# Ordering the engine queues of a linear-attention + MLP kernel with another scheduling model of the framework

## The chip, the cores and the metric

The kernel runs on one core of a Trainium2 chip. The metric is the device time of one execution, in microseconds (us). Before the change three runs gave 836.24, 839.51 and 843.57 us, a median of 839.51 us. The profile that is read below is of one more execution of the same kernel.

## The reference

Per batch and head (4 x 8 of them, head size 40) a 40 x 40 state is carried over 768 steps. The attention output then goes, as 3072 tokens of 320 numbers, through an MLP with 2048 hidden units and the function h * tanh(softplus(h)).

```python
for t in range(S):
    y[:, :, t] = np.einsum('bhd,bhde->bhe', rt, state)
    Sa = np.einsum('bhde,bhe->bhd', state, at)
    state_decay = state * wt[:, :, None, :] - np.einsum('bhd,bhe->bhde', Sa, bt)
    state = state_decay + np.einsum('bhd,bhe->bhde', vt, kt)
...
h = x @ w_in
g = h * np.tanh(softplus(h))
return g @ w_out
```

## The kernel before

The 768 steps are cut into 12 chunks of 64. Inside a chunk the recurrence becomes matrix products and the inverse of a triangular matrix, so that only the state goes from chunk to chunk. The text below uses these names:

- **P c.b** (`pre_a`, L128 to L203), the preparation of half b of chunk c, 24 in all. SyncE (SP) loads `wa` (L131) and `bk` (L134), each into one of two buffers, so P of two units later waits until the buffer is free. VectorE (DVE) forms running products of the decay: a reduction L145, a reciprocal L146, a scan L147, L150, L152, L156, a scan back L157, and L170, which scales `bk`. TensorE (PE) multiplies (L186) and transposes (L202); ScalarE (ACT) and DVE empty the results (L188 to L191, L193).
- **I n** (L209 to L220), the inversion for two chunks at a time, six in all, I0 to I5. It is one chain of 64 DVE instructions: a transpose L209, thirty pairs L214/L216, each of which needs the pair ahead of it, a transpose L218 that gives `TT`, and L220.
- **J n** (L232 to L260), what follows it on PE: 32 x 32 products L232 and L241, ACT copies into `bdT` (L249 to L251), and the products L258 that ACT copies into `KT` (L260). The chunks 2n and 2n+1 need J n.
- **a, b, u, d, c** of a chunk, the step itself, for two groups of heads: a is L277 to L286 (`pu`, with `KT`), b is L314/L316, u L293, d L304, and c is L334, L339 (`pq`), L342 and L346 (the new state) and L343 (the output `yev`).
- **W 0 to W 19**, the conversion of one piece of the MLP's weights. SP loads the piece into `cv_d` (L453), ACT makes `cv_m` (L459), DVE runs L461 to L463, ACT makes the high part `w_ih` or `w_oh` (L494) and DVE the low part `w_il` or `w_ol` (L495). W0 to W11 are `in_wi`, with one buffer for `cv_d` in all; W12 to W19 are `in_wo`. The last five, W15 to W19, have two buffers for `cv_d`.
- **X i** (L472 to L476, L565 to L568), the loads of MLP input i (`xy` and `xp`, one buffer each) and its split into `xh` (ACT, L566) and `xl` (DVE, L567, L568); **m i** (L583, L585, L588, L589), the first product of the MLP with its activation; **M i** (L603 to L605), the second product, which for token block 0 needs all of W12 to W19 in turn.

All of this is written in program order inside one `TileContext`. When the context is left, the framework's scheduler simulates the engines and decides the order in which each engine's instructions stand in its queue. Each engine then takes its queue strictly in that order; an instruction whose inputs aren't there holds up what is behind it, and so does a DMA issue on SP or POOL. The program gives the scheduler hints, `tc.high_priority(offset=...)`, from the table `OFF` for each piece of work:

```python
def at(tc, k):
    return tc.high_priority(offset=OFF[k]) if OFF.get(k) else nullcontext()
...
ORDER = '0aiA1'
```

`ORDER` is the program order for two chunks: step 2n, P of two pairs ahead, I and J of the next pair, at the end the weights, step 2n+1. Buffer counts (such as `NWA = 2` for `wa` and `bk`, `NXP = 1` for `xy` and `xp`, `CVC = 2` for the last `cv_d`) are constants at the head of the file.

Of the kernel before, what the change touches and what calls it, by code (L numbers as in the profile page):

```python
# [47 lines left out]
def layouts(inp, S=768):  # L48
    nch = S // C

    def v(x):
        return x[:, :, :S].reshape(4, 2, 2, 2, nch, C, 40)

    r, k, vv, w, a, b = (v(inp[n]) for n in 'rkvwab')
    o = {}
    wt = w.transpose(4, 2, 1, 6, 3, 0, 5).reshape(nch, 2, 2, 40, 8, C)
    wa = np.zeros(wt.shape[:4] + (1040,), np.float32)
    wa[..., :520].reshape(wt.shape[:4] + (8, 65))[..., 1:] = wt
    wa[..., 528:] = a.transpose(4, 2, 1, 6, 3, 0, 5).reshape(nch, 2, 2, 40, 512)
    o['wa'] = wa  # L60
    bt, kt = (x.transpose(4, 2, 1, 6, 3, 0, 5).reshape(nch, 2, 2, 40, 8, 1, C) for x in (b, k))
    bk = np.concatenate([bt, kt], -2)
    bk[:, 1] = np.concatenate([kt, bt], -2)[:, 1]
    o['bk'] = bk.reshape(nch, 2, 2, 40, 8, 128)
    o['rD'] = np.ascontiguousarray(r.transpose(4, 1, 6, 2, 3, 0, 5)).reshape(nch, 2, 40, 16, C)
    o['vD'] = np.ascontiguousarray(vv.transpose(4, 1, 6, 3, 0, 2, 5)).reshape(nch, 2, 40, 8, 128)
    o['vN'] = np.ascontiguousarray(vv.transpose(4, 2, 5, 3, 0, 1, 6)).reshape(nch, 2, C, 16, 40)
    p = np.arange(128)
    cst = np.zeros((128, 328), np.float32)
    cst[:, :128] = np.eye(128)  # L70
    cst[:, 128:192] = (p[:, None] % 64) < np.arange(64)
    cst[:, 192:256] = np.arange(64) < (p[:, None] // 64) * 32 + p[:, None] % 32
    cst[:, 256:296] = (p[:, None] % 64) == np.arange(40)
    cst[:, 296:328] = np.arange(32) < p[:, None] % 32
    o['cst'] = cst
    return o
# [356 lines left out]
def mlp_layouts(inp):  # L433
    wi, wo = inp['moe_w_in'], inp['moe_w_out']
    wi = wi.reshape(2, 2, 2, 40, 2048).transpose(1, 3, 0, 2, 4).reshape(320, 2048)
    a = np.empty((128, 3, 2048), wi.dtype)
    a[:, 0], a[:, 1] = wi[0:128], wi[128:256]
    a[0:64, 2] = a[64:128, 2] = wi[256:320]
    o = {'wi': a.reshape(128, 3, 4, 512).transpose(0, 2, 1, 3), 'wo': wo.reshape(16, 128, 320).transpose(1, 0, 2)}
    o = {n: np.ascontiguousarray(x).reshape(128, -1) for n, x in o.items()}  # L440

    return {n: x.view(np.int64) if x.dtype == np.float64 else x for n, x in o.items()}
# [185 lines left out]
def build(tc, I, out, nch):  # L628
    with ExitStack() as ctx:
        dp = ctx.enter_context(tc.tile_pool(name="dp", bufs=1, space=bass.MemoryType.DRAM))  # L630
        yD = dp.tile([nch, 2, 40, 2, 512], F32, name="yD")
        pD = dp.tile([nch, 2, 40, 2, 520], F32, name="pD")
        M = Mlp(ctx, tc, I, yD, pD, out)
        with ExitStack() as actx:
            attention(actx, tc, I, yD, pD, nch, M)
        M.run(nch)


def launch(**inputs):
    import concourse.bacc as bacc  # L640
    import concourse.tile as tile
    from concourse.bass_utils import run_bass_kernel_spmd

    nch = inputs['r'].shape[2] // C
    arrays = layouts(inputs, nch * C)
    arrays.update(mlp_layouts(inputs))
    nc = bacc.Bacc("TRN2", target_bir_lowering=False, num_devices=1)
    I = {n: nc.dram_tensor("in_" + n, x.shape, mybir.dt.from_np(x.dtype), kind="ExternalInput").ap() for n, x in arrays.items()}
    out = nc.dram_tensor("out_0", (nch * 256, 320), F32, kind="ExternalOutput").ap()
    with tile.TileContext(nc) as tc:  # L650
        build(tc, I, out, nch)
    res = run_bass_kernel_spmd(nc, [{"in_" + n: x for n, x in arrays.items()}], core_ids=[0]).results[0]["out_0"]
    return np.ascontiguousarray(res.reshape(nch, 4, C, 320).transpose(1, 0, 2, 3)).reshape(nch * 256, 320)
# [4 lines left out]
```

## Time and profile before

| | before |
|---|---|
| runs | 836.24, 839.51, 843.57 us |
| median | 839.51 us |
| profiled execution, first to last instruction | 843.5 us |
| PE, PEld, DVE, ACT, POOL busy | 748.6, 695.6, 462.0, 429.0, 103.3 us |
| mean granted TensorE clock | 0.939 |

The page gives no time of the profiled execution beside its span of 843.5 us. PE is the matmul part of TensorE and PEld its weight loads, which run beside the matmuls. An f32 matmul of the program leaves two records in the trace (the counts after x), one of the MLP, in another format, leaves one. In a timeline row the first number is the start in us, the second the length, and what stands in brackets is the idle time of the engine just before and what ended it. The table of stretches gives the busy time of each engine in it and then the clock that TensorE was granted (1.00 is full speed), the busy share of the DMA engines and GB/s.

### The profile page before, as it was taken

The page shows a single profiled execution, that of the slowest core. Times are in us where ns is not written, and L with a number is a line of the kernel's source. Part 1 is how long each engine was busy: PE and PEld are TensorE (multiplying, and loading weights), DVE is VectorE, ACT ScalarE, POOL GpSimd, SP SyncE. Part 2 cuts the span into 40 slices and gives each one's busy share as a digit, 9 for nine tenths or more (in the row PEclk, how much of TensorE's full clock was granted, in tenths as well). Part 3 has the DMA queues.
Part 4 walks back from the last instruction along what each step waited for, and adds up shares of the span by engine and source line. Part 5 has one row for each costly group of instructions (what it writes and reads, how often), then busy time and mean ns, then how long its engine had stood idle before and what let it go on. Part 6 is the DMA issues. An engine that isn't in the chain of part 4 may idle for free.

```text
span 843.5 us, 18796 instructions
## 1 busy us (share of the span) xinstructions
PE 748.6 (89%) x7816; PEld 695.6 (82%) x7816; DVE 462.0 (55%) x975; ACT 429.0 (51%) x937; POOL 103.3 (12%) x182
## 2 busy tenths in 40 slices
PE   2645898998989889889799899999999999999998
PEld 2534697887868778778768799999999999999998
DVE  6789879739899658788924639221222222122110
ACT  4533647774586866566738546333333333333331
POOL 8100012113122023221101200000000000000000
PEclk9855689899999999899959999999999999999999
DMA  6422223323423233323425734211120111100000
GB/s 177 134 71 64 74 63 73 90 67 105 129 81 80 66 88 103 82 67 96 123 66 142 179 109 128 54 35 36 38 54 25 31 54 35 35 21 16 16 1 32
DMA packets 58212, 61.91 MB, mean 73 GB/s; under 512 B 25536, under 2 KB 48704, under 8 KB 58128
## 3 DMA queue, kind: packets, MB, share of 16 engines
q1 hardware_dynamic: 49296, 40.94, 17.6%
q0 software_dynamic: 8832, 19.79, 9.5%
q8 instruction: 61, 1.00, 0.5%
q14 instruction: 23, 0.19, 0.1%
HBM read 48.79 MB, written 11.86 MB: 72 GB/s over the span
## 4 chain that ended last, share of the span: by engine, by line
PE 62%; DVE 15%; ACT 15%; issue 5%; DMA 2%; ACTq 0%; DVEq 0%; SPq 0%
PE ph L583 21%; PE po L604 7%; PE po L605 7%; PE po L603 7%; PE pa L186 5%; PE pa L258 4%; PE pq L314 3%; PE pq L334 2%; DVE XL L216 2%; DVE tmp L214 2%; ACT ad L155 2%; PE pu L284 1%; DMA cv_d<-in_wo 1%; DVE P L147 1%; ACT bdT L250 1%
## 5 line engine op out<-in xcount | busy, mean ns | idle before, releaser
L583 PE MATMUL ph<-xh,w_ih 128*128 128x256 f32 x576 | 148.3, 283 | 0.5 <-ACT xh L566 0.5
L585 ACT ACTIVATE g<-ph 128x512 f32<-128x512 f32 x96 | 57.3, 598 | 179.3 <-PE ph L583 179.2
L589 DVE TENSOR_TENSOR gl<-g,gh 128x1024 fp32r<-128x1024 f32 x48 | 58.7, 1225 | 160.7 <-ACT gh L588 160.4
L583 PE MATMUL ph<-xh,w_il 128*128 128x256 f32 x576 | 123.6, 283 | 0.0
L186 PE MATMUL pa<-bk,ad 128*128 128x168 f32 x384 | 85.0, 373 | 42.7 <-DVE bk L170 15.0
L604 PE MATMUL po<-w_ol,gh 128*128 128x320 f32 x384 | 118.8, 310 | 0.1
L605 PE MATMUL po<-w_oh,gl 128*128 128x320 f32 x384 | 118.4, 309 | 0.0
L603 PE MATMUL po<-w_oh,gh 128*128 128x320 f32 x384 | 117.7, 309 | 0.0
L186 PEld LDWEIGHTS pa<-bk,ad 128*128 128x128 f32 x384 | 70.8, 233 | 47.8 <-issue 22.8
L583 PEld LDWEIGHTS ph<-xh,w_ih 128*128 128x128 f32 x576 | 109.3, 190 | 0.7 <-ACT xh L566 0.7
L583 PE MATMUL ph<-xl,w_ih 128*128 128x256 f32 x384 | 101.2, 285 | 0.0
L583 PEld LDWEIGHTS ph<-xh,w_il 128*128 128x128 f32 x576 | 96.3, 190 | 0.0
L583 PEld LDWEIGHTS ph<-xl,w_ih 128*128 128x128 f32 x384 | 73.1, 190 | 0.8 <-issue 0.5
L604 PEld LDWEIGHTS po<-w_ol,gh 128*128 128x128 f32 x384 | 72.1, 188 | 0.5 <-DVE w_ol L495 0.5
L605 PEld LDWEIGHTS po<-w_oh,gl 128*128 128x128 f32 x384 | 72.1, 188 | 0.1
L603 PEld LDWEIGHTS po<-w_oh,gh 128*128 128x128 f32 x384 | 71.8, 188 | 0.0
L258 PE MATMUL pa<-bdT,HA 128*104 128x128 f32 x384 | 57.0, 304 | 9.0 <-ACT bdT L251 7.3
L258 PEld LDWEIGHTS pa<-bdT,HA 128*104 128x104 f32 x384 | 49.9, 190 | 14.4 <-ACT bdT L251 9.1
L216 DVE TENSOR_TENSOR XL<-XL,tmp 128x30 f32<-128x30 f32 (+9 forms) x180 | 59.0, 328 | 2.4
L214 DVE TENSOR_TENSOR tmp<-XL 128x30 f32<-128x30 f32 (+9 forms) x180 | 58.5, 325 | 2.5
L314 PE MATMUL pq<-bdr,UVT 128*128 128x128 f32 x384 | 57.3, 294 | 2.3 <-DVE UVQ L316 1.5
L314 PEld LDWEIGHTS pq<-bdr,UVT 128*128 128x128 f32 x384 | 50.8, 205 | 4.0 <-DVE UVQ L316 1.9
(89 smaller groups left out, 1243.5 us busy)
## 6 DMA issues: line engine op xcount, KB each, us to landing
wa<-in_wa SPq DMA_DIRECT2D x48, 162.5 KB
bk<-in_bk SPq DMA_DIRECT2D x48, 160.0 KB
cv_d<-in_wi SPq DMA_DIRECT2D x12, 512.0 KB
cv_d<-in_wo SPq DMA_DIRECT2D x8, 640.0 KB
pD<-P POOLq DMA_DIRECT2D x48, 81.2 KB, 2.2
VS<-in_vN POOLq DMA_DIRECT2D x24, 160.0 KB, 3.6
UVT<-in_vD POOLq DMA_DIRECT2D x24, 160.0 KB, 3.9
bdr<-in_rD POOLq DMA_DIRECT2D x24, 160.0 KB, 4.4
```

The source lines that it names most:

```text
L155: A.copy(ad[q, :, :, al], a[q].rearrange("p (s k t) -> p s k t", k=2, t=32))
L186: PE.matmul(pt[:, j], ad[:, s0 + j].rearrange("p k a t -> p (k a t)"), bk[:, s0 + j], start=(j == 0), stop=True, skip_group_check=True)
L214: V.tensor_tensor(out=tv, in0=X[:, i + 1:32, i:i + 1].broadcast_to([128, 31 - i, i]), in1=X[:, i:i + 1, 0:i].broadcast_to([128, 31 - i, i] ...
L216: V.tensor_tensor(out=X[:, i + 1:32, 0:i], in0=X[:, i + 1:32, 0:i], in1=tv, op=ALU.add)
L258: PE.matmul(pk[:, j], ha[:, s0 + j], bd[:, s0 + j].rearrange("p a t -> p (a t)"), start=(j == 0), stop=True, skip_group_check=True)
L314: PE.matmul(pq[:, s], UVT[:, g * 4 + s, be * 128:be * 128 + 128], br[:, be, g * 4 + s].rearrange("p a t -> p (a t)"), start=(s == 0), stop ...
L583: PE.matmul(o, w, x, start=(j == 0 and n == 0), stop=(n == 7), skip_group_check=True)
L585: A.activation(g[:, f0:f0 + 2], ph, AF.Mish)
L589: V.tensor_tensor(out=gl, in0=g, in1=gh.bitcast(F32), op=ALU.subtract)
L603: PE.matmul(po[k], gh[:, j, t], oh, start=(f == 0), stop=False, skip_group_check=True)
L604: PE.matmul(po[k], gh[:, j, t], ol, start=False, stop=False, skip_group_check=True)
L605: PE.matmul(po[k], gl[:, j, t], oh, start=False, stop=(f == 15), skip_group_check=True)
```

## The change

One argument is added where the context is opened. With it the scheduler times the engines with another simulation of the framework, a more detailed one, while it decides the order.

```diff
-    with tile.TileContext(nc) as tc:
+    with tile.TileContext(nc, schedule_with_timeline_sim=True) as tc:
         build(tc, I, out, nch)
```

The instructions stay the same: 5480 matmuls before and after, and the same counts on DVE and ACT. What moves is where they stand. Of PE's order 1661 rows differ, of ACT's 1293, of DVE's 989, of SP's 89, of POOL's 38. The larger part of the difference is local: on each engine the same pieces follow each other in nearly the same sequence, and are interleaved in another way. From the fourth token block of the MLP on, PE's order is the same.

On DVE, up to the end of I0 (its L218), 18 instructions stand ahead that stood behind it: L170 of P 4.0, the eight from L145 to L170 of P 4.1, six of P 5.0 (L145 to L156), L145 of P 5.1, and the last L191 and L193 of P 3.1. Ahead of the first instruction of I0 (L209) there are P 2.0 through L170 and three of P 2.1, where before only the first two of P 2.0 stood there. On PE the six L186 of P 4.0 and the last two L202 of P 3.1 now stand ahead of J 0.

**DVE at the last inversion, I5, which chunk 10 and 11 wait for.** Rows from 805 of the queue before (`cv_w_5108` is W7, `cv_w_5118` W8) and the rows around the same L218 now (`cv_w_5130` is W9).

```order
L461 TENSOR_SCALAR cv_w_5108<-cv_m_5111 128x512
L216 TENSOR_TENSOR XL_4746<-XL_4746,tmp_4827 128x4x27
L462 SCALAR_TENSOR_TENSOR cv_w_5108<-cv_m_5111,cv_w_5108 128x512
L214 TENSOR_TENSOR tmp_4830<-XL_4746 128x84
L463 SCALAR_TENSOR_TENSOR cv_w_5108<-cv_d_5109,cv_w_5108 128x512
L316 TENSOR_TENSOR UVQ0_119<-pq_5182,cst_95 128x8x64
L216 TENSOR_TENSOR XL_4746<-XL_4746,tmp_4830 128x3x28
```

```order
L214 TENSOR_TENSOR tmp_4836<-XL_4746 128x30
L461 TENSOR_SCALAR cv_w_5130<-cv_m_5133 128x512
L216 TENSOR_TENSOR XL_4746<-XL_4746,tmp_4836 128x30
L462 SCALAR_TENSOR_TENSOR cv_w_5130<-cv_m_5133,cv_w_5130 128x512
L218 STREAM_TRANSPOSE TT_4839<-XL_4746 128x32x32
L463 SCALAR_TENSOR_TENSOR cv_w_5130<-cv_d_5131,cv_w_5130 128x512
L220 STREAM_TRANSPOSE GP_3855<-TT_4839 64x32x32
L316 TENSOR_TENSOR UVQ0_119<-pq_5182,cst_95 128x8x64
```

Between the first instruction of I5 and its L218 there stood five conversions, W3 to W7; now there stand six whole ones, W3 to W8, and L461 and L462 of W9. The first L461 (W3) comes after 3 pairs of I5 instead of after 8. The two L316 of chunk 9, first group (`pq_5182` and its partner), stood ahead of L218 and now stand behind L220.

**PE behind it, where J5 and c of chunk 9 share the engine.** The L258 are J5's, the L334 and L339 chunk 9's.

```order
L258 MATMUL pa_4917<-bdT0_103,HA_3856 104x128
L334 MATMUL pq_5282<-UVQ1_120,bkn_3157 64x104
L339 MATMUL pq_5282<-bdr0_121,smd_5206 64x2x64
L258 MATMUL pa_4923<-bdT0_103,HA_3856 104x128
L339 MATMUL pq_5282<-bdr0_121,smd_5206 64x2x64
```

```order
L304 MATMUL pu_5258<-cst_95,ST1_123 128x128 x4
L314 MATMUL pq_5239<-bdr0_121,UVT_118 128x128
L258 MATMUL pa_4917<-bdT0_103,HA_3856 104x128 x4
L258 MATMUL pa_4923<-bdT0_103,HA_3856 104x128 x4
L334 MATMUL pq_5282<-UVQ0_119,bkn_3093 64x104
L334 MATMUL pq_5282<-UVQ1_120,bkn_3157 64x104
```

Before, six of these L258 stood singly between single products of c; now eight follow each other. Just ahead of this place the L241 of J5 alternate singly with L334 and L339 twelve times before and ten times now. The array shape (32, 64 or 128 columns per tile) changes 254 times between neighbours in PE's whole order before, and 217 times now.

**SP at the start of the MLP.** The rows that issue X3's and X4's loads (`xy_6400`, `xp_6401` and `xp_6685`) and the last conversions' loads, before and now.

```order
L473 DMA xp_6401<-pD_58 128x4x64 x2
L476 DMA xp_6401<-pD_58 64x4x64 x2
L453 DMA cv_d_5787<-in_wo 128x1280
L453 DMA cv_d_5799<-in_wo 128x1280
L472 DMA xy_6400<-yD_57 128x256 x2
L475 DMA xy_6400<-yD_57 64x256 x2
L453 DMA cv_d_5811<-in_wo 128x1280
```

```order
L472 DMA xy_6400<-yD_57 128x256 x2
L475 DMA xy_6400<-yD_57 64x256 x2
L473 DMA xp_6685<-pD_58 128x4x64 x2
L476 DMA xp_6685<-pD_58 64x4x64
L453 DMA cv_d_5787<-in_wo 128x1280
L453 DMA cv_d_5799<-in_wo 128x1280
L476 DMA xp_6685<-pD_58 64x4x64
L453 DMA cv_d_5811<-in_wo 128x1280
```

The loads of W15 and W16 stood ahead of X3's `xy`; now they stand behind it and behind three of X4's `xp` loads, which need X3's product L565 to have read `xp`. On DVE, L565 of X3 moves with them: it now stands right behind X2's L568, ahead of the first L589, where before it stood behind the first conversions.

## The prediction

> **What bounds the kernel now.** First the head of the page, then the stretches.
>
> ```profile
> span 843.5 us, 18796 instructions
> PE 748.6 (89%) x7816; PEld 695.6 (82%) x7816; DVE 462.0 (55%) x975; ACT 429.0 (51%) x937; POOL 103.3 (12%) x182
> ```
>
> ```profile
> 0.00:50.00 50.00, 24.52 (x112) 21.01 (x112) 34.56 (x68) 25.46 (x65) 19.55 (x36) 0.86 0.51 141
> 50.00:100.00 50.00, 26.72 (x144) 22.10 (x144) 46.40 (x116) 19.82 (x58) 5.07 (x10) 0.62 0.24 70
> 100.00:500.00 400.00, 357.59 (x5002) 313.57 (x4998) 289.21 (x696) 257.07 (x633) 78.73 (x136) 0.94 0.36 93
> 430.00:440.00 10.00, 9.90 (x44) 6.11 (x43) 2.83 (x5) 3.49 (x8) 1.56 (x2) 0.50 0.32 85
> 500.00:530.00 30.00, 29.89 (x223) 29.35 (x222) 23.90 (x30) 19.96 (x29) 0.00 (x0) 1.00 0.47 137
> ```
>
> The columns are PE, PEld, DVE, ACT, POOL, clock, DMA share, GB/s. Three stages show. Up to 100 us PE is idle for half of the time, while DVE is busy for 34.6 and then 46.4 of 50 us: DVE sets the pace. From 100 to 500 us PE is busy for 357.6 of 400 us, so 42.4 us are idle. From 500 us on PE has no gap (29.89 of 30 us), and its order there is the same from the fourth token block on. A new order adds no work, so the time can change in three ways only: PE's idle time up to 530 us, its clock, and what changing between unlike matmuls costs it.
>
> What ends DVE's first stage is inversion I0; PE takes J0 at once when `TT` is there.
>
> ```profile
> 49.87 2.09 DVE L209 STREAM_TRANSPOSE XL<-GP 128x1024 f32<-128x1024 f32 x1
> ```
> ```profile
> 97.25 1.93 DVE L218 STREAM_TRANSPOSE TT<-XL 128x1024 f32<-128x1024 f32 x1
> ```
> ```profile
> 99.24 1.82 PE L232 MATMUL pa<-TT,GP 32*32 32x32 f32 x64 [0.24 <-DVE TT L218]
> ```
>
> **Term 1, the start: +1.5 us.** The groups of DVE in the first 100 us price the instructions that now stand ahead of L218.
>
> ```profile
> L157 DVE TENSOR_TENSOR_SCAN wa<-wa,d 128x519 f32<-128x519 f32 x9 | 11.1, 1236 | 3.8 <-ACT ad L155 3.8
> L147 DVE TENSOR_TENSOR_SCAN P<-wa,d 128x520 f32<-128x520 f32 x9 | 11.1, 1233 | 0.1
> L170 DVE TENSOR_TENSOR bk<-bk,wa 128x1024 f32<-128x1024 f32 x8 | 9.8, 1220 | 0.1
> L191 DVE TENSOR_TENSOR HA<-pa,cst 128x192 f32<-128x192 f32 (+1 forms) x24 | 8.0, 331 | 9.6 <-ACT HA L190 9.6
> L152 DVE TENSOR_TENSOR wa<-wa,P 128x512 f32<-128x512 f32 x9 | 6.2, 684 | 0.0
> L145 DVE TENSOR_REDUCE w<-wa 128x8 f32<-128x256 f32 x9 | 3.7, 411 | 0.0
> ```
>
> Of the 18, ten are of these forms: two L170 (2.44), two L147 (2.47), one L157 (1.24), two L152 (1.37), three L145 (1.23) make 8.7 us. The last L191 is 0.3, and for each of the seven small ones I take 0.2, an estimate below that L191: 10.4 us in all. Some 6.6 us of it stands ahead of L209 (the rest of P 2.0, 4.7, and the first three of P 2.1, 1.8), where DVE was busy for 34.6 of 50 us; 3.8 us comes between L209 and L218, where it was nearly full. Of the idle 15.4 us, 9.6 + 3.8 us (up to 100 us) are DVE waiting for ACT inside one P; work of the next P, put into those waits, costs nothing. So L209 comes at about the same time and `TT` some 4 us later. Against that PE has six L186 and two L202 behind it; sixteen records of L186 or L202 took 1.97 to 4.85 us in this stage, so I credit 2.5 us. Bounds: if nothing hides, +10.4 - 2.5 = +8; if the better interleaving also empties another 6 us of DVE's waits, 4 - 6 - 2.5 = -4.5. I take +1.5, nearer to the waits that the L191 row shows.
>
> **Term 2, the last inversion: +5 us.** In the same way I5 ends what PE waits for before J5.
>
> ```profile
> 367.63 1.93 DVE L218 STREAM_TRANSPOSE TT<-XL 128x1024 f32<-128x1024 f32 x1
> ```
> ```profile
> 381.57 0.43 DVE L461 TENSOR_SCALAR cv_w<-cv_m 128x512 int32<-128x512 int32 x1
> ...
> 416.15 2.02 DVE L218 STREAM_TRANSPOSE TT<-XL 128x1024 f32<-128x1024 f32 x1
> 418.02 0.41 DVE L461 TENSOR_SCALAR cv_w<-cv_m 128x512 int32<-128x512 int32 x1
> ```
> ```profile
> 391.58 5.02 DMA cv_d<-in_wi
> ```
> ```profile
> 376.11 72.58 SPq L453 DMA_DIRECT2D cv_d<-in_wi  x9
> ```
>
> From W3's L461 to W8's (five conversions) it is 36.45 us, 7.3 us each: `cv_d` has one buffer, so a load (5.02 us here) starts only when the L463 ahead of it is done. That pace was just covered by DVE's own work. Now six cycles lie between W3's L461 and W9's, and L218 stands behind W9's L462: 6 x 7.3 + 0.4 + 0.7 + 2.0 = 46.9 us from W3's L461 to the end of `TT`, against 418.17 - 381.57 = 36.6 before: 10.3 us more. Part is given back: before, W3's load was issued at 376.11, 6.5 us after the `TT` of I4 (369.56), since P 11.1 held its memory until PE's last L202; now all of P 11.1 stands ahead of J4 on PE, so the load can go some 4 to 5 us sooner. That leaves +5 to +6; I take +5. What is queued behind L461 on DVE when it waits is I5 itself and the L316 and L342 of chunk 8, for which PE waits too. Bounds: 0, if the loads land sooner than in the row, and +10.
>
> **Term 3, alternating matmuls: -6 us there, -1.5 us elsewhere.** The timeline of PE around 420 us:
>
> ```profile
> 400.86 0.93 PE L334 MATMUL pq<-UVQ,bkn 128*64 128x104 f32 x16 [0.30 <-ACT yev L343]
> ...
> 404.61 1.99 PE L258 MATMUL pa<-bdT,HA 128*104 128x128 f32 x16 [1.64 <-ACT bdT L251]
> ...
> 421.39 0.82 PE L241 MATMUL pa<-X,GP 32*32 32x32 f32 x40 [0.65 <-ACT X L235]
> 422.14 0.39 PE L334 MATMUL pq<-UVQ,bkn 128*64 128x104 f32 x2
> ...
> 422.64 0.39 PE L334 MATMUL pq<-UVQ,bkn 128*64 128x104 f32 x2
> ...
> 425.17 0.61 PE L334 MATMUL pq<-UVQ,bkn 128*64 128x104 f32 x2
> ...
> 425.95 0.61 PE L334 MATMUL pq<-UVQ,bkn 128*64 128x104 f32 x2
> ...
> 434.20 0.76 PE L258 MATMUL pa<-bdT,HA 128*104 128x128 f32 x2
> ...
> 435.42 0.76 PE L258 MATMUL pa<-bdT,HA 128*104 128x128 f32 x2
> ```
>
> In a run, two records of L334 cost 2 x 0.93/16 = 0.12 us and two of L241 0.04 us. Alternating, such a pair takes 422.64 - 422.14 = 0.50 us, so one change of shape costs (0.50 - 0.16)/2 = 0.17 us. At half clock the pair takes 0.78 us. L258 with L334 takes 1.22 us, against 0.25 + 0.12 = 0.37 in runs (0.73 at half clock). Two alternations fewer of the first kind save 1.2 us, six fewer of the second 6 x (1.22 - 0.73) = 2.9 to 6 x (1.22 - 0.37) = 5.1 us: 4.1 to 6.3, and up to 2 us more for what follows if the clock comes back sooner: I take 6. PE was the last to be waited for here (in 430 to 440 us DVE was busy for 2.83 of 10). Of the 37 changes of shape saved in all some 20 lie here; the other 17 x 0.17 = 2.9 us count half, since other engines are on the path there as often. Bounds for the term: -10, and 0 if the wait of term 2 sets the end of this stretch.
>
> The clock needs a word. It was granted at 0.50 in 430 to 440 us although PE counts as busy for 9.90 of 10 us: the alternation itself looks idle to the gate. The Trainium skill (TensorE: Matmul & The Clock Gate, Part 1: The HAM clock gate) says that the clock is halved after an idle window of about 3.4 us and comes back after a busy one of that length. The trace differs in that no wait of that length stands in the timeline there. By that rule a wait of 5 us for `TT` would halve the clock ahead of J5, and this term would come to nothing; it is a rival below.
>
> **Term 4, the start of the MLP: +3.7 us.** X2 ends when m of block 0 has let go of `xh`, at 501.1 us, and the last weights follow.
>
> ```profile
> 501.19 0.83 ACT L566 CAST xh<-xy 128x768 fp32r<-128x768 f32 x1 [3.24 <-PE ph L583]
> ```
> ```profile
> 500.85 0.81 SPq L453 DMA_DIRECT2D cv_d<-in_wo  x2
> 503.27 0.80 SPq L472 DMA_DIRECT2D xy<-yD  x2
> ...
> 534.11 0.80 SPq L472 DMA_DIRECT2D xy<-yD  x2
> ...
> 538.83 1.23 SPq L473 DMA_DIRECT2D xp<-pD  x2
> ```
> ```profile
> 511.06 0.83 DVE L495 SCALAR_TENSOR_TENSOR w_ol<-cv_w,w_oh 128x640 fp32r<-128x640 f32 x1
> ...
> 526.65 0.82 DVE L495 SCALAR_TENSOR_TENSOR w_ol<-cv_w,w_oh 128x640 fp32r<-128x640 f32 x1
> ...
> 537.84 0.96 DVE L565 TENSOR_TENSOR xy<-xy,xp 128x768 f32<-128x768 f32 x1 [2.54 <-DMA xy<-yD]
> ```
>
> Before, W15 and W16 were issued at 500.85 and the weight was there at 511.9, 11 us later; W19 followed at 527.5. PE had no gap, but the last of the five was only just in time. Now the issue stands behind X3's `xy` (503.27), its landing and L565 (537.84 - 534.11 = 3.7 us after the issue, 0.96 long), and three `xp` issues (1.9 us): 503.3 + 3.7 + 1.0 + 1.9 = 509.9, 9 us later. Waiting less for DVE, W15 needs 9 to 11 us from there: 7 to 9 us later, and W19 as much, so at 534.5 to 536.5. PE has more to fill with: its order puts 63 m instead of 39, and half of c of chunk 11, between the end of m of block 0 and the first use of W15, 24 x 0.12 + 1.9 = 4.8 us. So 2.2 to 4.2 us stay as a gap, and in the first of them DVE also holds back L589 behind the waiting L565. I take +3.7. Bounds: 0, if c of chunk 11 and X3 come early enough, and +6.
>
> **The sum.** +1.5 + 5 - 6 - 1.5 + 3.7 = +2.7 us on the profiled 843.5. That execution is like the slowest of the three runs and 4 us above their median, so on the median it is 839.5 + 2.7 = 842 us. What is not priced is the rest of the new interleaving between 100 and 370 us; with 42.4 us of idle PE in 100 to 500 us I give it +-7, a sixth.
>
> **The rivals.** *Faster, 825 us.* PE's path sets the end everywhere: the start costs nothing (-2.5), the loads of term 2 land in time (0), the alternation gives its 10 with the clock back, elsewhere 2.9, and m covers the late weights (+1): -14.4. For it: PE is busy for 89% of the span and DVE for 55%. Against it: each inversion's `TT` was waited for, and DVE takes its queue in order.
>
> *Slower, 852 us.* One mechanism, at I5: the weight loads pace DVE. `TT` comes the full 10 us late, PE stands, its clock is halved when J5 starts, and the 6 us of the alternation aren't seen: +1.5 + 10 + 0 - 1.5 + 3.7 = +13.7, less 1 us because W10 and W11 are then ahead. It decides when `TT` comes 8 us or more late against the `TT` of I4. For it: the 7.3 us cycle in the rows is steady. Against it: W3 may start 4 us sooner.
>
> *The order is only another of equal worth, within 3 us of 839.5.* The terms then cancel with the unpriced part; it lies within my forecast.
>
> **How the numbers follow.** A measurement of this kernel, whose three runs lie 7.3 us apart, can tell about 1% (8.4 us) from no change. The forecast, 842 us with its own range of 834 to 850, has 0.48 within 1% together with the last rival. Faster by over 1% (below 831) has 0.24: the faster rival, and the unpriced part. Slower by over 1% (above 848) has 0.28: the slower rival, and term 1 at its upper bound. The range that holds it 8 times in 10 reaches into both: 826 to 857.
>
> **What would show it.** In the profile after: `TT` of I0 (the first L218) ending between 97 and 107 us, L209 near 50. From the L218 of I4 to that of I5 52 to 55 us instead of 48.5, with DVE idle at L461 waiting for `cv_m`, 1 to 3 us at a time, and L461 still 7 us apart. From J5's first L232 to u of chunk 10 about 6 us less on PE. L453 of W15 issued 8 to 9 us after X2's L566, and a gap of PE of 2 to 5 us at L603 to L605 near 515 to 535 us. The prediction is wrong at its root if PE's idle time between 100 and 370 us changes by more than 7 us, or if the first `TT` comes later than 110 us.

## The result, and the profile after

Four runs of the changed kernel gave a median of 894.41 us (886.28 to 897.46), beside 840.97 us for the kernel before on the same chip: a ratio of 1.064, 95% interval 1.059 to 1.069. The prediction had 842 us and a range up to 857. The profiled execution took 884.5 us, 41.0 us more than the profiled one of before.

The head of the page after the change:

```profile
span 884.5 us, 18829 instructions
PE 747.8 (85%) x7816; PEld 703.9 (80%) x7816; DVE 465.8 (53%) x975; ACT 426.3 (48%) x937; POOL 103.4 (12%) x182
```

The counts of matmuls and of DVE's and ACT's instructions are those of before; PE's busy time is 0.8 us less, DVE's 3.8 us more. So nearly all of the loss is idle time. The stretches after (columns PE, PEld, DVE, ACT, POOL, clock, DMA share, GB/s):

```profile
0.00:50.00 50.00, 22.34 (x100) 18.57 (x100) 33.71 (x68) 24.06 (x59) 20.46 (x38) 0.83 0.50 137
50.00:100.00 50.00, 31.25 (x136) 26.06 (x136) 39.17 (x92) 22.23 (x66) 5.08 (x10) 0.73 0.29 87
100.00:150.00 50.00, 26.64 (x445) 24.73 (x446) 41.15 (x106) 19.00 (x46) 5.27 (x8) 0.69 0.09 25
150.00:500.00 350.00, 292.94 (x4174) 263.69 (x4172) 243.13 (x589) 217.87 (x557) 68.62 (x121) 0.91 0.34 87
```

From 50 to 100 us DVE is busy for 39.17 us where it was busy for 46.40: the engine that sets the pace has begun to wait. PE's loss shows later: in 100 to 150 us it works for 26.64 of 50 us, where before it worked for 45.64:

```profile
100.00:150.00 50.00, 45.64 (x607) 40.87 (x603) 42.44 (x111) 32.35 (x81) 8.71 (x16) 0.87 0.28 68
```

What it waits for there is the first `TT`:

```profile
117.78 1.91 DVE L218 STREAM_TRANSPOSE TT<-XL 128x1024 f32<-128x1024 f32 x1
119.74 1.49 PE L232 MATMUL pa<-TT,GP 32*32 32x32 f32 x48 [19.72 <-DVE TT L218]
```

What DVE waits for is seen when its groups of both kernels are laid side by side. First before, then after; the last part of a row is the idle time ahead of these instructions and what ended it:

```profile
L145 DVE TENSOR_REDUCE w<-wa 128x8 f32<-128x256 f32 x24 | 9.9, 410 | 0.5 <-PE pa L166 0.4
L170 DVE TENSOR_TENSOR bk<-bk,wa 128x1024 f32<-128x1024 f32 x24 | 29.1, 1214 | 0.1
```

```profile
L145 DVE TENSOR_REDUCE w<-wa 128x8 f32<-128x256 f32 x24 | 10.0, 418 | 40.9 <-DMA wa<-in_wa 40.9
L170 DVE TENSOR_TENSOR bk<-bk,wa 128x1024 f32<-128x1024 f32 x24 | 29.2, 1218 | 21.1 <-DMA bk<-in_bk 19.7 <-PE pq L314 1.3
```

DVE now waits 60.6 us for the loads of P, `wa` and `bk`, where before it waited for none. One cycle of it, in DVE's timeline and then in SP's, between the two waits:

```profile
72.32 1.21 DVE L170 TENSOR_TENSOR bk<-bk,wa 128x1024 f32<-128x1024 f32 x1
...
80.69 0.42 DVE L145 TENSOR_REDUCE w<-wa 128x8 f32<-128x256 f32 x1 [3.15 <-DMA wa<-in_wa]
81.03 1.23 DVE L157 TENSOR_TENSOR_SCAN wa<-wa,d 128x519 f32<-128x519 f32 x1
...
83.23 1.21 DVE L170 TENSOR_TENSOR bk<-bk,wa 128x1024 f32<-128x1024 f32 x1
...
90.50 0.42 DVE L145 TENSOR_REDUCE w<-wa 128x8 f32<-128x256 f32 x1 [2.91 <-DMA wa<-in_wa]
```

```profile
73.86 1.66 SPq L134 DMA_DIRECT2D bk<-in_bk  x2
75.63 0.84 SPq L131 DMA_DIRECT2D wa<-in_wa  x2
84.83 0.78 SPq L134 DMA_DIRECT2D bk<-in_bk  x1
85.79 0.78 SPq L131 DMA_DIRECT2D wa<-in_wa  x2
```

L170 ends at 73.5 and lets go of one `wa`. SP issues two `bk` loads that stand ahead, then `wa` at 75.63, and 5.1 us after this issue L145 can start. The reduction itself takes 0.4 us, but L157 and L170 of the P ahead stand behind it in DVE's queue, ready and held up; and this L170 is what lets go of the other `wa`. So a P costs a load and half its own work in turn, 9.8 us from L145 to L145. What stands behind it all, the pairs of I0 and with them `TT`, pays for each. The Trainium skill (DMA: Bandwidth & Descriptors, Anatomy of one DMA — SWDGE (gpsimd) path) fits 2.0 us plus the bytes at 436 GB/s for one transfer issued by GpSimd; for one of a P's two `wa` loads, 162.5 KB, that would be an estimate of 2.4 us. Here the two loads, issued by SP behind two `bk` loads on the same queue, took about twice that, 5.1 us.

The order alone shows where L145 went. For 23 pairs of neighbouring P, the new order has L145 of the next P ahead of L157 of the P before it 21 times, and ahead of its L170 23 times; the order of before 9 and 14 times. But the place alone does not decide, since those 9 did not wait for a load either. What tells the two orders apart is the time from the end of the L170 that frees a `wa` to the L145 that needs it: before, 5.5 to 14.5 us passed there, in which the load could land; in the change 19 of the 22 later L145 waited, and began 3.7 to 7.8 us after that L170.

The ends of the six `TT` (from L218 of I0 to I5) are the milestones of all that follows, in us, each from its profiled execution:

| | I0 | I1 | I2 | I3 | I4 | I5 | end |
|---|---|---|---|---|---|---|---|
| before | 99.2 | 151.9 | 235.8 | 278.4 | 369.6 | 418.2 | 843.5 |
| after | 119.7 | 156.2 | 263.5 | 300.4 | 409.5 | 459.4 | 884.5 |
| new order, three buffers | 107.1 | 143.4 | 245.5 | 283.6 | 381.2 | 433.9 | 861.5 |
| old start, new rest, three buffers | 96.9 | 140.4 | 241.0 | 275.4 | 372.3 | 424.7 | 850.9 |
| new start, old rest | 122.2 | 172.6 | 256.5 | 299.4 | 392.6 | 440.9 | 859.0 |
| old start, new rest | 95.9 | 143.1 | 253.5 | 289.7 | 401.0 | 451.6 | 880.4 |
| before with early L145 | 111.5 | 172.7 | 268.0 | 312.3 | 413.0 | 460.6 | 880.9 |
| before to I4, new end | 101.9 | 154.5 | 238.4 | 281.0 | 370.6 | 427.6 | 854.0 |
| before, grouped products | 97.9 | 147.8 | 230.2 | 272.9 | 364.2 | 412.1 | 824.6 |

The change is 39.9 us late at the fifth `TT`, 41.2 at the sixth and 41.0 at the end. Up to the fifth, DVE's busy time is the third number of these stretches of before, after, and the new order with three buffers:

```profile
0.00:369.56 369.56, 290.91 (x3616) 255.76 (x3616) 293.44 (x714) 222.81 (x584) 84.03 (x154) 0.89 0.34 89
```
```profile
0.00:409.50 409.50, 298.69 (x3640) 266.03 (x3640) 299.19 (x719) 225.53 (x598) 85.93 (x156) 0.86 0.31 82
```
```profile
0.00:381.20 381.20, 296.20 (x3640) 264.50 (x3640) 299.08 (x720) 225.27 (x599) 87.04 (x157) 0.86 0.33 88
```

Busy 293.4, 299.2, 299.1; idle 76.1, 110.3, 82.1. So of the 39.9 us, 5.8 are DVE work that the new order puts ahead of this `TT`, and 34.2 are DVE's idle time.

### The profile page after: what moved, and what is told of

Its sections match the earlier page's. It is cut to its first block, busy times and chain, and to the rows that moved or that the text cites. A ratio compares the mean times of both kernels' runs of the same rounds, so it can differ in the third digit from the quotient of the medians.

```text
span 884.5 us, 18829 instructions
## 1 busy us (share of the span) xinstructions
PE 747.8 (85%) x7816; PEld 703.9 (80%) x7816; DVE 465.8 (53%) x975; ACT 426.3 (48%) x937; POOL 103.4 (12%) x182
## 4 chain that ended last, share of the span: by engine, by line
PE 58%; DMA 12%; DVE 12%; ACT 9%; issue 4%; SPq 2%; POOL 0%; DVEq 0%; ACTq 0%
PE ph L583 21%; PE po L605 6%; PE po L603 6%; PE po L604 6%; DMA wa<-in_wa 5%; DMA bk<-in_bk 4%; PE pq L314 3%; PE pa L186 3%; DVE XL L216 3%; DVE tmp L214 3%; PE pa L202 3%; PE pa L258 2%; DMA cv_d<-in_wi 2%; PE pq L334 2%; PE pa L241 1%
## 5 line engine op out<-in xcount | busy, mean ns | idle before, releaser
L589 DVE TENSOR_TENSOR gl<-g,gh 128x1024 fp32r<-128x1024 f32 x48 | 58.6, 1225 | 161.8 <-ACT gh L588 161.5
L186 PE MATMUL pa<-bk,ad 128*128 128x168 f32 x384 | 86.9, 381 | 37.4 <-DVE bk L170 17.3
L186 PEld LDWEIGHTS pa<-bk,ad 128*128 128x128 f32 x384 | 73.2, 240 | 43.3 <-DVE HA L191 19.6
L202 PE MATMUL pa<-cst,bk 128*128 128x128 f32 x192 | 37.2, 328 | 25.2 <-DVE HA L191 18.1
L334 PE MATMUL pq<-UVQ,bkn 128*64 128x104 f32 (+1 forms) x768 | 47.4, 263 | 11.6 <-DVE UVQ L316 6.2
## 6 DMA issues: line engine op xcount, KB each, us to landing
wa<-in_wa SPq DMA_DIRECT2D x48, 162.5 KB
```

Source lines behind the costliest of these rows:

```text
L186: PE.matmul(pt[:, j], ad[:, s0 + j].rearrange("p k a t -> p (k a t)"), bk[:, s0 + j], start=(j == 0), stop=True, skip_group_check=True)
L202: PE.transpose(pt[:, j].rearrange("p a b -> p (a b)"), bk[:, s0 + j, 0:128], ident)
L334: PE.matmul(py[be * 64:be * 64 + 64, 2 * j + al, 0:n], BKN[c, be][:, u * 40:u * 40 + 64], UVQ[be][:, u, 0:n], start=(j == 0 and al == 0), ...
L589: V.tensor_tensor(out=gl, in0=g, in1=gh.bitcast(F32), op=ALU.subtract)
```

## The experiments

The theories. **A:** DVE's waits for the loads of `wa` and `bk`, made by where L145 stands, are the loss. **B:** the work ahead of each `TT` is, and waits only fill time that is idle anyway. **D:** all comes from the late start. **E:** the waits for loads take the place of waits for PE and ACT (these fell by 26 us up to the fifth `TT`), which would come back. **G:** the end of the program holds more than the traces say. **H:** the interleaving of the middle is worse in itself.

To change one thing and keep the rest, the kernels of the experiments trace the program, let the scheduler order it, read its order, edit it, trace the program anew and give the scheduler the edited order as edges that mean only "issued behind":

```python
order = traced(nch, arrays, schedule_with_timeline_sim=True)[1]   # or without it: the order of before
q = queues(order)                                                 # one list for each engine, edited here
for queue in q.values():
    for a, b in zip(queue, queue[1:]):
        tc.add_manual_dep(b, a.name, NoSync)
```

**1. The first ten L145 put back.**

```diff
+for n in range(1, 11):
+    here = d.index((L170, V, n))
+    late = [k for k in d[:here] if k[2] == n + 1 and k[0] in (L145, L146, L147, L150, L152, L156)]
+    d[:here + 1] = [k for k in d[:here + 1] if k not in late] + late
```

In these ten pairs the new order has only L145, and in four of them L146, ahead of that L170, so that no more than these move.

> The new order on every engine, with one edit on DVE: for the first ten pairs of neighbouring P, L145 and L146 of the next P stand behind L170 of the P ahead of them, instead of in front of its L157 and L170. Theory A (loads): the next P's L145 waits for a `wa` load that can start only when an earlier L170 is done, and L157 and L170 behind it are held up for nothing; each P then has a load in its cycle. DVE's waits for `wa` and `bk` ahead of the first TT (13 us) fall below 5 us, the first TT ends at 109 to 113 us instead of 119.7, and the total falls by 4 to 10 us against the change's 894. Theory B (work): the first TT is late because of the work that stands ahead of it, not because of waits; it stays within 3 us of 119.7 and the total within 4 us of 894.

885.0 us beside 844.4: 1.051 (1.044 to 1.059), against 1.064 for the change. The first `TT` ended at 110.8. The waits for loads ahead of it, 21.7 us in the change over the whole start (13.8 of them from 40 us on), came to 4.6. As A has it, and not B.

**2. The same for all pairs.** From the eleventh on nearly the whole first half of the next P stood ahead of L170, and is moved behind it.

```diff
-for n in range(1, 11):
+for n in range(1, 24):
```

> As the run with ten pairs, but for all 23 pairs, and with everything of the next P from L145 to L156 that stood ahead of L170 of the P before it moved behind that L170. Theory A (loads): DVE's waits for the two loads over the whole span fall from 60.6 us to below 30, and the total to 860 to 880 us. Theory B (work): the waits move elsewhere, the total stays within 8 us of 894.

906.1 us, 1.075 (1.069 to 1.080): slower than the change, so what A expected here failed; B's number, within 8 us of 894, is missed as well. The groups of DVE say where it went:

```profile
L170 DVE TENSOR_TENSOR bk<-bk,wa 128x1024 f32<-128x1024 f32 x24 | 29.3, 1223 | 46.1 <-DMA bk<-in_bk 41.5 <-PE pa L258 3.7 <-DVE HA L191 0.9
L145 DVE TENSOR_REDUCE w<-wa 128x8 f32<-128x256 f32 x24 | 9.9, 413 | 2.4 <-DMA wa<-in_wa 2.4
```

The wait for `wa` is gone and that for `bk` has doubled: L170 waits for it, and now the next P's half, which could have run meanwhile, stands behind. So L145's place is not the whole of it: with two buffers each, whatever waits for a load must have work ahead of it.

**3 and 4. The new order up to the first `TT` and that of before for the rest, and the other way round.**

```diff
+first = new[:new.index((L218, V, 1)) + 1]                  # run 4: old
+order = first + [k for k in old if k not in set(first)]    # run 4: new
```

> The new order up to the first TT (the L218 of I0), the order of before for all that is left. Theory A (loads in every stage): the first TT comes at 118 to 122 us as in the change, but the work done ahead of it is taken off what follows, as in the change, where the second TT was only 4 us late; the total is 845 to 862 us. Theory D (start alone): the late start is kept to the end, and nothing later matters: 855 to 865 from 20 us of delay, and with the recovered part lost again up to 885.

> The order of before up to the first TT, the new order for all that is left. Theory A (loads in every stage): the first TT comes at 99 us, DVE still waits 30 to 45 us for the two loads after it, and the total is 860 to 880 us. Theory D (start alone): 838 to 850 us, with DVE's later waits off the path.

Run 3: 867.1 us, 1.026 (1.020 to 1.033). Run 4: 882.5 us, 1.045 (1.038 to 1.052). Run 4 speaks against D: with the first `TT` at 95.9 the fifth is again 31 us late, and DVE waits 41.8 us for the loads after all, as A had it; its time is 2.5 us above A's range. Run 3 misses A's 845 to 862 and lies within D's reach, which went up to 885. The order of before does not make up for the late start, as A had assumed: the second `TT` is 20.7 us late, where in the change it was 4.3, the fifth 23.0, and the end 15.5. So the start does cost on its own, and so does the rest; the two losses make 7.1% together, no clear difference from 6.4 within their intervals.

**5 and 6. Three buffers for `wa` and `bk`, each order kept.**

```diff
-NWA = 2
+NWA = 3
...
-    m = pool.tile([128, n], I32, name="cv_m")
+    m = hi
```

> The new order on every engine, word for word, with three buffers instead of two for each of `wa` and `bk` (the memory for it comes from the weight conversion, whose `cv_m` is written over the upper half of `cv_d`), so that a load can start one P earlier. Theory A (loads): DVE's 61 us of waiting for the two loads fall below 12, DVE's idle time up to the fifth TT falls from 110 us towards the 76 of before, and the total is 845 to 865 us (the 6 us of work that the new order puts ahead of that TT stay). Theory E (the waits for loads only stand where DVE would have waited for PE or ACT anyway, since these waits fell by 26 us): they come back, the total is 870 to 890 us.

> The order of before on every engine with the same three buffers, as a control. Theory A and E alike: DVE waits for no `wa` or `bk` in before, so the total stays within 1% of it; theory A's gain in the run with the new order is then due to the pairing of that order with two buffers.

Run 5: 861.3 us beside 840.9, 1.022 (1.019 to 1.025). Run 6: 845.2 us, 1.004 (1.001 to 1.006). With the new order, word for word, the two groups are now

```profile
L170 DVE TENSOR_TENSOR bk<-bk,wa 128x1024 f32<-128x1024 f32 x24 | 28.9, 1202 | 0.0
L145 DVE TENSOR_REDUCE w<-wa 128x8 f32<-128x256 f32 x24 | 9.7, 406 | 1.9 <-DMA wa<-in_wa 1.9
```

and 4.2 of the 6.4% are gone. The order of before gains nothing from the same buffers. That is A's forecast. E is right in part: up to the fifth `TT` the 60.6 us of waits for loads, all of which lie ahead of it, were worth 28.3 us (409.5 - 381.2), for other waits came back.

**7 and 8. Three buffers, ordered anew by each model.**

```diff
 NWA = 3
-    with tile.TileContext(nc) as tc:
+    with tile.TileContext(nc, schedule_with_timeline_sim=True) as tc:    # run 7 alone
```

> Three buffers for `wa` and `bk`, and the scheduler orders anew with the more detailed model. Theory A: if the model takes a load to be there sooner than the chip brings it, it again starts each P too close behind the buffer's release, now one P later; with three buffers DVE waits below 30 us and the total is 840 to 870 us. Theory E: 870 to 895 us.

> Three buffers for `wa` and `bk`, ordered anew by the model of before. Theory A: 835 to 850 us, since before has no wait for these loads to lose; a gain of over 1% would say that the two buffers cost something in before that isn't seen as a wait for a load.

Run 7: 857.8 us, 1.019 (1.017 to 1.021), with 9.3 us of waiting for `wa`. Run 8: 861.5 us, 1.023 (1.020 to 1.026), where A expected no loss. So the model of before, too, gives an order that is 2% slower once something around it changes: of the orders tried, the one of before is good by more than its model. Why the more detailed model puts L145 where it does is not settled by these runs.

**9 to 11. Only the end of the program in the new order:** from the fifth `TT` on; from there to the last new state (L346 of chunk 10); and from the sixth `TT` to that state.

```diff
+for part, last in ((old, [(L218, V, 5)]), (new, None)):           # run 9
+for part, last in ((old, [(L218, V, 5)]), (new, L346), (old, None)):   # run 10
+for part, last in ((old, [(L218, V, 6)]), (new, L346), (old, None)):   # run 11
+    order += [k for k in part[:max(part.index(k) for k in last) + 1] if k not in set(order)]
```

> The order of before up to the fifth TT (the L218 of I4), the new order for all that is left: I5 with the weight conversions, J5, the last three chunks and the MLP, so the terms 2, 3 (its larger part) and 4 of the prediction alone. By the prediction's terms +5 - 6 + 3.7: 842 to 848 us against 840 to 843 of before. By the two traces (fifth to sixth TT 1.3 us longer, from there to the last new state 6.2 shorter, from there to the end 6 longer): within 4 us of before. Theory G (the order of the end holds more of the change's 41 us than the traces say, since what it lost was hidden behind the late start): 850 us or more.

> The order of before up to the fifth TT, the new order from there to the last new state (L346 of chunk 10), then the order of before again, the MLP among it: terms 2 and 3 without term 4. By the prediction's terms +5 - 6: within 2 us of before. By the two traces (+1.3 - 6.2): 4 to 6 us below before, 0.5 to 0.7%. Theory G: not faster.

> The order of before up to the sixth TT (the L218 of I5), the new order from there to the last new state, then the order of before again: term 3 alone, where eight L258 of J5 follow each other instead of standing singly between the L334 of chunk 9. By the prediction's term: 4 to 6 us below before, 834 to 838 us, and the clock at half speed for at most 7 us after the sixth TT instead of 20.5. Theory G: not faster, because what PE saves there it waits for at the start of the MLP.

Run 9: 856.8 us beside 844.2, 1.018 (1.013 to 1.023). Run 10: 853.1 us, 1.013 (1.008 to 1.018). Run 11: 852.1 us, 1.012 (1.008 to 1.017). G has it for all three; the forecasts by the prediction's terms and by the two traces fail in each. For runs 9 and 10 the reason can be seen at W3. In run 9 the sixth `TT` comes 57.0 us after the fifth instead of 48.6, and DVE's timeline shows the pace of the weight loads as the prediction had it:

```profile
381.36 0.43 DVE L461 TENSOR_SCALAR cv_w<-cv_m 128x512 int32<-128x512 int32 x1 [1.64 <-ACT cv_m L459]
...
424.59 0.43 DVE L461 TENSOR_SCALAR cv_w<-cv_m 128x512 int32<-128x512 int32 x1 [1.87 <-ACT cv_m L459]
425.66 1.94 DVE L218 STREAM_TRANSPOSE TT<-XL 128x1024 f32<-128x1024 f32 x1
```

Six cycles in 43.2 us, 7.2 each, and 46.2 us from the first L461 to the end of `TT`. W3's load was issued at 376.3 here, 5.7 us behind I4's `TT`; in the change, whose `TT` came late, it was issued at 409.0, half a microsecond ahead of it, and the same conversions cost little. In run 11 the sixth `TT` is on time, but from it to the last new state (the end of the last L346) it takes 69.0 us instead of 63.9. PE's timeline there:

```profile
416.75 1.79 PE L232 MATMUL pa<-TT,GP 32*32 32x32 f32 x64 [1.61 <-DVE TT L218]
...
427.02 1.39 PE L241 MATMUL pa<-X,GP 32*32 32x32 f32 x44 [4.46 <-ACT X L235]
430.60 0.62 PE L334 MATMUL pq<-UVQ,bkn 128*64 128x104 f32 x4 [2.19 <-DVE UVQ L316]
431.15 0.31 PE L241 MATMUL pa<-X,GP 32*32 32x32 f32 x2
431.39 0.61 PE L334 MATMUL pq<-UVQ,bkn 128*64 128x104 f32 x2
```

PE waits 4.46 us for ACT's L235, and that wait is the change's own mechanism again, on another engine. In ACT's queue the conversion L459 stands ahead of J5's copies; it waits for a weight load, and the copies, whose `TT` ended at 416.7, begin only behind it, at 422.56:

```profile
422.00 0.66 ACT L459 ACTIVATE cv_m<-cv_d 128x512 f32<-128x512 f32 x1 [2.94 <-DMA cv_d<-in_wi]
```

So G's reason for run 11, waits at the start of the MLP, is not what happened: from the last new state to the end it takes 362.0 us, before 361.4. The alternating products behind the wait run at half clock, 0.78 us a pair. The clock was at one half from 417 to 444 us (in the row of this stretch, PE's 20.35 us busy are followed by PEld, DVE, ACT, POOL and then the clock):

```profile
417.00:444.00 27.00, 20.35 (x188) 16.04 (x182) 11.54 (x18) 10.88 (x24) 1.48 (x2) 0.50 0.22 69
```

**12. Three buffers for `wa` alone.**

```diff
-wa, bk, ad = wab[n % NWA], bkb[n % NWA], adb[n % 2]
+wa, bk, ad = wab[n % 3], bkb[n % 2], adb[n % 2]
```

> The new order on every engine with three buffers for `wa` alone; `bk` keeps two. Theory A: DVE's 41 us of waiting for `wa` fall below 15; the wait for `bk` (20 us) stays or grows, since its buffer is free only when PE's last L202 of two P ago is done and its issue also holds up the `wa` issue behind it on SP; total 868 to 885 us, between the change and the run with three of both (861). If it comes out at 861 as well, `bk` never mattered; at 890 or more, `wa` alone buys nothing.

881.2 us, 1.046 (1.041 to 1.051). The wait for `wa` is 10.6 us, that for `bk` 23.5. Both loads count: the third `wa` alone brings 1.8 of the 4.2% that the two together brought. SP waited 118.9 us at L134, whose `bk` is freed by PE's L202, against 75.8 in the change, and the issues of `wa` stand behind it in SP's queue. A third buffer for `bk` alone was not run.

**13. Alternating products put together, on the order of before.** PE's queue alone is edited, at five places.

```diff
+pair = {out[q[i]], out[q[i + 1]]}                # two tiles whose single products alternate from i to j
+q[i:j] = sorted(q[i:j], key=lambda k: out[k] != out[q[i]])
```

> The order of before, with PE's queue alone edited: at five places where single products of two tiles alternate, those of one tile stand behind those of the other (53 changes of tile fewer, 33 of them at J5 and chunk 9). By the prediction's term 3 (0.17 us a change at full clock, 0.25 at half, and the clock back sooner): 6 to 10 us below before. Theory G (what PE saves at J5 it waits for later, as in the run with the new order after I5): within 3 us of before.

825.7 us beside 841.8, 0.983 (0.979 to 0.987): faster than both kernels, and by more than was expected. PE's timeline behind the sixth `TT`, and the stretches from there to the last new state of before, after, run 11 and this run:

```profile
415.33 1.20 PE L241 MATMUL pa<-X,GP 32*32 32x32 f32 x64 [0.65 <-ACT X L235]
416.46 0.93 PE L334 MATMUL pq<-UVQ,bkn 128*64 128x104 f32 x16
417.23 0.61 PE L339 MATMUL pq<-bdr,smd 128*64 128x128 f32 x8
```

```profile
418.00:482.00 64.00, 59.57 (x738) 47.95 (x738) 30.68 (x55) 37.41 (x77) 9.15 (x13) 0.84 0.46 118
```
```profile
459.00:517.00 58.00, 52.16 (x773) 46.16 (x773) 28.33 (x50) 36.92 (x77) 8.44 (x13) 0.95 0.48 125
```
```profile
416.00:485.00 69.00, 56.16 (x734) 48.39 (x735) 30.89 (x54) 37.84 (x78) 6.98 (x10) 0.78 0.41 108
```
```profile
412.00:463.00 51.00, 45.11 (x738) 39.91 (x738) 30.48 (x55) 37.27 (x77) 9.18 (x13) 1.00 0.59 148
```

The first number behind the length is PE's busy time, the sixth the clock. PE needs 45.1 us for what took it 59.6, the clock does not fall in this stretch, and it is 13 us shorter. The other 6 us of this run came before the sixth `TT` (412.1 instead of 418.2).

Not all of the 13 us is the grouping. In this stretch runs 3 and 15 have PE's order of before, alternating products and all, and there the clock hardly fell. The same rows of these two:

```profile
440.90:497.70 56.80, 51.30 (x738) 42.69 (x738) 30.42 (x54) 37.44 (x77) 9.10 (x13) 1.00 0.53 133
```
```profile
460.60:519.40 58.80, 52.79 (x738) 43.69 (x738) 30.60 (x55) 37.44 (x77) 9.50 (x13) 0.97 0.51 129
```

The same order takes 63.9 us in the profile of before and 56.9 in that of run 3. By these profiles, one of each run, some 7 of the 13 us come with the clock, and 6 are left for the changes of shape: 33 of them at the prediction's 0.17 us are 5.6.

**14. The start of before, then the new order, with three buffers.**

```diff
+first = old[:old.index((L218, V, 1)) + 1]
+order = first + [k for k in new if k not in set(first)]
...
-NWA = 2
+NWA = 3
```

> The order of before up to the first TT, the new order for all that is left, and three buffers each for `wa` and `bk`. What is left of the change's loss with three buffers (861 against 841) should be the P work put ahead of the first TT and of the fifth (6 us of DVE) and the end of the program (9 to 12 us by the run with the new end). Theory A (loads, then work ahead, then the end): no waits for loads, first TT at 99 us, 850 to 858 us. Theory H (the interleaving of the middle is worse in itself, loads or not): 860 us or more.

854.4 us beside 841.8, 1.017 (1.011 to 1.022). No wait for `wa` or `bk` is left on DVE. It lies in A's range and below H's. Beside run 5, 10.6 us of 18.0 are gone in the profiles: that is the work put ahead of the first `TT` (96.9 instead of 107.1). What remains against the profile of before is 2.7 us at the fifth `TT`, 3.8 more at I5, 3.5 less from there to the last new state and 4.3 more to the end; in the medians it is 12.5 us.

**15. The mirror of run 1: only L145 put early, on the order of before.**

```diff
+for n in range(1, 24):
+    if d.index((L145, V, n + 1)) > d.index((L157, V, n)):
+        d.remove((L145, V, n + 1))
+        d.insert(d.index((L157, V, n)), (L145, V, n + 1))
```

> The order of before on every engine, with one edit on DVE, the mirror of the one tried on the new order: wherever the next P's L145 stood behind L157 of the P ahead of it (14 of 23 pairs), it now stands directly in front of that L157, as in the new order. Theory A (loads): waits for `wa` appear on DVE, 10 to 40 us in all, and the total grows by 5 to 25 us. Theory B (work): the same work stands ahead of every TT, so the total stays within 4 us of before.

882.7 us beside 841.8, 1.051 (1.046 to 1.056). Fourteen instructions of 0.4 us, put earlier in one queue, cost 41 us, and eight of them waited for their load:

```profile
L145 DVE TENSOR_REDUCE w<-wa 128x8 f32<-128x256 f32 x24 | 9.9, 412 | 38.6 <-DMA wa<-in_wa 38.0 <-PE pa L166 0.4
```

It is more than A expected in time, and as much in waits. B, which had no change here, is out: one instruction more stands ahead of the first `TT` (181 instead of 180).

## Why the prediction was wrong

**What bounds the kernel.** DVE's pace in the first 100 us was read rightly, and that PE takes J0 as soon as `TT` is there. From "a new order adds no work" I went on to PE's idle time, its clock and its changes; that DVE's own queue could begin to wait for DMA was in none of the three.

**Term 1, the start, is the step that failed.** It had +1.5 us, at most +8; the first `TT` came 20.5 us later. The sentence that failed is that work of the next P, put into DVE's waits, costs nothing. The waits for ACT were indeed filled (9.6 us at L191 became 1.4), and DVE's work ahead rose by 8.8 us (10.4 forecast). But the first instruction of the next P needs a load whose buffer the P before it has just let go of, and I costed the moved instructions by their durations and not by when their inputs can be there. SP's part in it, the issue of L131 and L134, I did not cost at all. Without the waits for loads (run 5) the first `TT` ends at 107.1, 7.9 us late: the upper bound of the term as it stood.

**The unpriced rest, +-7 us between 100 and 370, was 19.4 us** (from the first to the fifth `TT`, 289.8 instead of 270.4), by the same mechanism: 39 us of waits for loads after the first `TT`. The criteria given for "wrong at its root" were met, both of them: PE's idle time from 100 to 370 us went from 30.0 to 57.3 us, and the first `TT` came at 119.7. The three-buffer runs and the mirror make this cause shown and not only argued. They do not bring back all: with three buffers 2.2 of the 6.4% stay.

**Term 2, the weight loads at I5.** The mechanism and the pace were right: 7.2 us a cycle and 46.2 us to the end of `TT` in run 9, where 7.3 and 46.9 stood in the working. That run lost 8.4 us there. In the change itself it was only 1.3: against I4's `TT` W3's load came 7 us sooner than before, and the credit for that had been put at 4 to 5. A credit of 7 would still leave 3 of the 10.3; where the other 2 went is not known. In runs 5 and 14, without the delay by loads ahead of it, the stage lost 4.1 and 3.8 us, near the forecast's 5.

**Term 3, alternating products.** -6 us was forecast at J5, and from the sixth `TT` to the last new state the change took 58.2 us instead of 63.9, 5.7 less. That the number agrees is luck. With PE's order of before, runs 3 and 15 took 56.9 and 58.7 us there, and run 6, also with that order, 64.0: what parts them is the clock (1.00, 0.97 and 0.84 of full speed in this stretch), and the new order at 0.96 is no better than the old one at full clock. With the new order the stretch is 4.4 us shorter than before in run 9 and 5.1 longer in run 11. The price of a change of shape holds: the pairs of L241 and L334 that are left take 0.49 us, and run 13 gained by it what that price says. (The 1.2 us in the working for two alternations sets a pair at half clock against a run at full; at one and the same clock two are worth 0.7 to 0.9.)

"Alternation itself looks idle to the gate" does not stand: runs 3 and 15 have the same alternation with the clock up. The rival in which PE waits for a late `TT` and the clock then eats the gain is not borne out: in run 9 `TT` came 8.4 us late against I4's, the clock was down from 422.8 us but up again 2 us behind `TT` (429.6), and the gain was there; in run 11 `TT` was on time and the gain was not. The Trainium skill (TensorE: Matmul & The Clock Gate, Part 1: The HAM clock gate) has the clock halved after an idle window of some 3.4 us. Run 11's wait of 4.46 us does not explain its half clock by that rule, for the clock fell at 417.0 and the wait began at 422.6.

**Term 4, the start of the MLP.** +3.7 forecast; from the last new state to the end the change took 5.5 us more, and runs 9 and 10, which have different orders only there, differ by 5.3 us in it. The size is near, the mechanism was wrong. L453 of W15 was issued 10.2 us after X2's L566 (8 to 9 forecast), but no product waited for it. PE's two large gaps are these:

```profile
504.87 0.74 PE L583 MATMUL ph<-xh,w_ih 128*128 128x256 f32 x4 [2.89 <-ACT xh L566]
```
```profile
544.48 0.41 PE L603 MATMUL po<-w_oh,gh 128*128 128x320 f32 x1 [3.21 <-ACT gh L588]
```

The first lies ahead of the last new state (517.6), and run 10, with the MLP in the order of before, has one like it (3.57 us), so it is not part of this term. The second waits for ACT's L588, for which the profile names the write of the attention's last output:

```profile
543.38 2.94 ACT L588 CAST gh<-g 128x1024 fp32r<-128x1024 f32 x3 [4.52 <-DMA yD<-yev]
```

Behind this gap the clock is at one half for 3.4 us (546.5 to 549.9). Run 9 has both (2.75 us, and 514.9 to 518.3), run 10 neither.

**The rivals.** The slower one had the right sign and a wrong place: it put the loss at I5, by the weights' loads, and 852 us. The same kind of event, an in-order queue that runs up against a buffer's release, happened at nearly every P.

What stays open: why the more detailed model puts L145 so close behind the release, and what makes the clock fall, and stay down, at J5 in some runs and not in others.

## What to carry to other kernels

When a scheduler reorders in-order queues, look first, for each instruction that waits for a load, at how much work stands on its engine between the instruction that frees the buffer and the one that needs the next load; the sum of durations says nothing on it. For `wa` DVE had 2.3 to 11.1 us of work there before, and 0.3 to 5.2 us after. A short instruction with a late input, put ahead of ready work, costs its wait times everything behind it: 14 reductions of 0.4 us cost 41 us here. And orders of the same instructions differ by 2% with hardly a wait for these loads in them (runs 5, 8 and 14), so one that is cheap to edit by hand, like products grouped by shape (1.7% here), is worth trying before another model.

## What the runs showed of the hardware that was not expected

Alternation alone does not halve the clock. Stretches of alternating products, in before and then in the change:

```profile
424.00:444.00 20.00, 19.90 (x92) 13.18 (x91) 4.32 (x9) 5.96 (x15) 1.56 (x2) 0.50 0.16 43
```
```profile
467.00:473.00 6.00, 6.00 (x72) 3.94 (x65) 1.21 (x3) 1.09 (x3) 0.00 (x0) 1.00 0.31 90
```

In before they ran at half clock for 20 us, in the change ten pairs of L241 and L334 or L339 ran at full clock, 0.49 us for one with L334, and PE counts as fully busy in both. The same twelve pairs in the order of before ran at full clock, too, in runs 3 and 15. In run 11 the clock was down for 27 us. With the clock, one and the same stretch of PE's order went from 56.9 us (run 3) to 63.9 (before), about as much as grouping its products saves at full clock.

The two `wa` loads of a P took 5.1 us from their issue to their use behind two `bk` loads on the same queue, and a third buffer for `wa` alone was worth only 1.8% of the 6.4: SP's waits at L134 for a free `bk` grew from 75.8 to 118.9 us, and `wa` is issued behind them.
